# Attention scores in three fp32r products of high and low parts, split on GpSimd, in a fused attention and feed-forward kernel

## The chip, the cores and the metric

One Trainium2 chip, one core. The metric is device time in microseconds of one execution, the median of several runs. Lower is better.

## The reference

Attention with a position bias for 4 batches, 8 heads, 576 positions and 64 features a head, followed by a feed-forward layer with a rational activation. All inputs and the output are float32 in shape and meaning (the feed-forward weights arrive as 64-bit numbers and are converted in the kernel). Cut to what matters here:

```python
scores = scale * np.matmul(q, k.transpose(0, 1, 3, 2))      # (4, 8, 576, 576)
...
scores = scores + bias.transpose(2, 0, 1)[None, :, :, :]
scores = scores - np.max(scores, axis=-1, keepdims=True)
attn = np.exp(scores)
attn = attn / (np.sum(attn, axis=-1, keepdims=True) + 1e-09)
attn_out = np.matmul(attn, v)
...
h = x @ w_in
...
out = g @ w_out                                              # g: a ratio of polynomials of h
```

## The kernel before, in words

The program has two halves. In the first, to about 260 us, the bias table is built (to about 44 us) and then attention is computed. In the second the feed-forward layer runs on TensorE in fp32r, each float32 operand split into a high part (rounded to fp32r) and a low part (the rest), with three products: high by high, high by low, low by high.

Attention is cut into 16 units: a unit is a pair of heads of one batch (`units`). The two heads of a pair lie in the two halves of the 128 partitions, 64 features each. A unit has four blocks of 128 query rows (c = 0 to 3, the full blocks), and the last 64 rows of two neighbouring units share a fifth block (c = 4). So two units make nine steps, and there are 72 steps (`steps`). In the order of one group, counted by the step's number modulo nine, steps 0 to 3 are full blocks of the even unit, step 4 is the shared short block, and 5 to 8 are full blocks of the odd unit. The change concerns `e_qk`, which multiplies q by k for one step: for each half a of the key columns (288 each) and each head j one `T.matmul` in float32 with 64 rows of contraction. A float32 matmul appears in the trace as two records. Each head's scores go to a PSUM tile of their own (`sc`, two tiles in all, so every step uses both again).

What a step issues is written out by hand in `step_a(i)`, engine by engine and in order:

- TensorE: the scores of step i (`e_qk`, L337), the transposes of the exponentials of step i-2 (`e_tp`, L406, and of the sums, L422), the products with v of step i-3 (`e_pv`, L446).
- VectorE: two reductions of step i (`e_ttr`, L347, one per head: adds the bias, scales, finds the extreme, and so empties the score tiles), then, where a unit ends, the sums' reciprocals (`e_recip`, L373 and L374), copies out of PSUM (L425, L429, L456), and one operation of the background job.
- ScalarE: the exponentials (L363) and the copy of the transposes out of PSUM (L414), and one operation of the job.
- GpSimd: the normalization `e_norm` (L395, two in nine steps) and two operations of each job.

The background job converts one block of feed-forward weights (`w_conv`): VectorE masks (`mag`, L140, SBUF to SBUF with a constant), ScalarE rebiases (L149), VectorE puts the sign in (`sign`, L152, two tensors from SBUF) and joins the mantissa (`join`, L165, two tensors from SBUF), GpSimd copies 16-bit halves (`mid`, L161) and subtracts the high from the joined value (`low`, L172, after `join`). `run_jobs` hands out one VectorE operation a step from step 8 on, and with it whatever follows it in the list for the other engines, so a job takes three steps; twenty jobs run in the stage. With L140 handed out in steps 2, 5 and 8 of a group, VectorE runs it after the scores of the next step have started: L140 in steps 0, 3 and 6, L152 in 1, 4 and 7, L165 in 2, 5 and 8.

Each engine runs its instructions in the order of issue. DMAs are issued from SP, in order too. `loads(i)` issues the loads of q and k (`load_qk`): those of the even unit of the next group in step 0, of the odd one in step 5.

Of the kernel before, what the change touches and what calls it, by code (L numbers as in the profile page):

```python
# [8 lines left out]
F32 = mybir.dt.float32  # L9
F32R = mybir.dt.float32r  # L10
U32 = mybir.dt.uint32
AF = mybir.ActivationFunctionType
ALU = mybir.AluOpType
# [3 lines left out]
P = 128  # L17
# [12 lines left out]
SH = S // 2  # L30
# [3 lines left out]
def tile_attn_moe(  # L34
# [79 lines left out]
    def w_conv(f, part):  # L114
        st = {}
        here = f < 6
        eng = G if f < KF - LATE else V

        def load():
            w = (w_in, w_out)[part]  # L120

            def get(nm, o, src):
                t = stg.tile([P, 4 * FN + 4], U16, tag="wx", name=f"{nm}{f}_{part}", bufs=3)
                nc.sync.dma_start(out=t[:, o:o + 4 * FN], in_=src)
                return t

            x = get("wx", 0, w.bitcast(U16)[f])[:, 0:4 * FN]
            st["u"] = x.bitcast(U32).rearrange("p (f t) -> p f t", t=2)[:, :, 1]
            if eng is G:
                st["h"] = x.rearrange("p (f t) -> p f t", t=4)[:, :, 1:3]  # L130
            else:
                y = get("wy", 1, w.bitcast(U16)[f])[:, 2:4 * FN + 2]
                st["m"] = y.bitcast(U32).rearrange("p (f t) -> p f t", t=2)[:, :, 0]

        def tl(nm, dt, bufs=1):
            st[nm] = stg.tile([P, FN], dt, tag=nm, name=f"{nm}{f}_{part}", bufs=bufs)
            return st[nm]

        def mag():
            V.tensor_scalar(  # L140
                out=tl("wk", U32), in0=st["u"], scalar1=0x7FFFFE00, scalar2=None, op0=ALU.bitwise_and
            )

        def rows(t):
            return t.rearrange("p (k f) -> p k f", k=KD)

        def rebias():
            st["wh"] = rows(tl("wh", U32, 2))
            A.activation(out=st["wh"], in_=rows(st["wk"]), func=AF.Relu, bias=wmin, scale=8.0)  # L149

        def sign():
            V.scalar_tensor_tensor(  # L152
                out=st["wh"], in0=rows(st["u"]), scalar=0x80000000, in1=st["wh"],
                op0=ALU.bitwise_and, op1=ALU.bitwise_or,
            )

        def mid():
            if eng is G:
                st["m"] = tl("wm", U32)
                m = st["m"].bitcast(U16).rearrange("p (f t) -> p f t", t=2)  # L160
                G.tensor_copy(out=m, in_=st["h"])  # L161

        def join():
            st["x"] = st["m"] if eng is G else tl("wk", U32)
            V.scalar_tensor_tensor(  # L165
                out=rows(st["x"]), in0=rows(st["m"]), scalar=13, in1=st["wh"],
                op0=ALU.logical_shift_right, op1=ALU.bitwise_or,
            )

        def low():  # L170
            st["wl"] = w_hilo(f, part)[1] if here else rows(tl("wl", F32R, 2))
            eng.tensor_tensor(  # L172
                out=st["wl"], in0=rows(st["x"]).bitcast(F32), in1=st["wh"].bitcast(F32), op=ALU.subtract
            )

        def store(hi=True, lo=True):
            if not here:
                w_out_to(f, part, st["wh"] if hi else None, st["wl"] if lo else None)
            elif hi:
                nc.sync.dma_start(out=w_hilo(f, part)[0].bitcast(F32), in_=st["wh"].bitcast(F32))  # L180

        return [load, [mag], [rebias], [sign, join, low, store], mid]

    def w_plain(f, part):
        st = {}

        def load():
            st["x"] = stg.tile([P, KD, P], F32, tag="wx", name=f"wx{f}_{part}")
            nc.sync.dma_start(out=st["x"], in_=w_src(f, part))

        def hi():
            st["h"] = stg.tile([P, KD, P], F32R, tag="wh", name=f"wh{f}_{part}")
            A.copy(out=st["h"], in_=st["x"])

        def lo():
            st["l"] = stg.tile([P, KD, P], F32R, tag="wl", name=f"wl{f}_{part}")
            V.tensor_tensor(out=st["l"], in0=st["x"], in1=st["h"].bitcast(F32), op=ALU.subtract)

        return [load, [], [hi], [lo, lambda: None, lambda hi=True, lo=True: w_out_to(f, part, st["h"] if hi else None, st["l"] if lo else None)], lambda: None]
# [31 lines left out]
    with tc.manual_schedule():  # L231
# [3 lines left out]
        with ExitStack() as actx:  # L235
# [9 lines left out]
                G.memset(t, 0.0)  # L245

            units = [(p, b) for p in range(NP) for b in range(B)]
            qk = {}
            vt = {}
            bias = {}  # L250

# [10 lines left out]
            def load_qk(u, eng=nc.sync):  # L262
                p, b = units[u]
                q = qkp.tile([P, S], F32, tag="q", name=f"q{u}", bufs=3)
                k = qkp.tile([P, S], F32, tag="k", name=f"k{u}", bufs=3)
                eng.dma_start(out=q, in_=qt[b, p])
                eng.dma_start(out=k, in_=kt[b, p])
                qk[u] = (q, k)

            def load_v(u, eng=nc.sync):  # L270
                p, b = units[u]
                t = vpool.tile([P, 5, P], F32, tag="v", name=f"v{u}")
                eng.dma_start(out=t, in_=vp[b, p])
                vt[u] = t
# [49 lines left out]
            def e_qk(i):  # L324
                u, c = steps[i]
                for j in range(2):
                    sc[i, j] = ps_sc.tile([P, 2, 512], F32, tag="sc", name=f"sc{i}_{j}")
                if c < 4:
                    ops = [(u, slice(c * P, c * P + P), slice(0, P))]
                else:  # L330
                    ops = [(u + z, slice(512, S), slice(64 * z, 64 * z + 64)) for z in range(2)]
                for a in range(2):
                    for j in range(2):
                        r = slice(64 * j, 64 * j + 64)
                        for n, x, o in ops:
                            q, k = qk[n]
                            T.matmul(  # L337
                                sc[i, j][o, a, :SH], q[r, x], k[r, a * SH:(a + 1) * SH],
                                start=True, stop=True,
                            )  # L340

            def e_ttr(i, j):
                u, c = steps[i]
# [54 lines left out]
            def e_tp(i, mx):  # L398
# [16 lines left out]
                last = c == (3 if u % 2 else 4)  # L415
                if last:
                    n = nsum(u)
                    rt = epool.tile([10, P], F32, tag="rt", name=f"rt{u}", bufs=2)
                    rsum[u] = dpool.tile([n, P], F32, tag=f"rs{u}", name=f"rs{u}")
                    for r in range(2):  # L420
                        x = slice(64 * r, 64 * r + 64)
                        T.transpose(mx[:, r, 64:P], sums[u % 4][x, :], ident[x, x])  # L422
# [58 lines left out]
            def loads(i):  # L481
# [5 lines left out]
                        load_v(u)  # L487
                if i == UPG + 1:
                    load_v(3)
                p, r = divmod(i, 2 * UPG)  # L490
                r = {2: 0, 7: 1, 11: 2, 13: 3, 16: 4}.get(r)
                if r is not None and p + 1 < NP:
# [465 lines left out]
```

## Time and profile before

| what | value |
|---|---|
| median of 3 runs | 671.99 us (671.89 to 672.24) |
| span of the profiled execution | 669.7 us |
| busy: TensorE matmul | 663.3 us (99%) |
| busy: VectorE | 569.1 us (85%) |
| busy: ScalarE | 481.7 us (72%) |
| busy: GpSimd | 156.5 us (23%) |
| attention steps | about 44 to 260 us, 2.97 to 3.08 us each |

The span runs from the first to the last instruction that the profiler shows; the device time of the runs holds a little more at either end. A busy share is a mean over the whole span; the attention stage has other shares than the feed-forward half. Records of matmuls are pipelined: the start of one to the start of the next is its price, not its length.

### The profile page before, as it was taken

How to read it: one execution, taken by the hardware profiler on the slowest of the kernel's cores; microseconds unless marked ns; L12 is line 12 of the kernel's file. 1: busy time of each engine (PE TensorE's matmuls, PEld its weight loads, DVE VectorE, ACT ScalarE, POOL GpSimd, SP SyncE). 2: the span in 40 equal slices, each digit the busy share in tenths (PEclk: the TensorE clock that was granted, in tenths of full speed). 3: DMA queues.
4: the chain of work that ended last, by engine and by line, in shares of the span. 5: the costliest groups of instructions: out<-in, count | busy, mean ns of one | idle time of the engine just before them, and what ended most of it. 6: DMA issues, size and time to landing. Idle time of an engine off the chain costs nothing.

```text
span 669.7 us, 16638 instructions
## 1 busy us (share of the span) xinstructions
PE 663.3 (99%) x6466; PEld 574.2 (86%) x6466; DVE 569.1 (85%) x1068; ACT 481.7 (72%) x769; POOL 156.5 (23%) x116
## 2 busy tenths in 40 slices
PE   9999999999999999999999999999999999999997
PEld 6657888888888888999999999999999999999995
DVE  7996888888888895799999999998978787878776
ACT  7978988989898996767676666666655555555561
POOL 0000233334334321122222222222222222222221
PEclk9999999999999999999999999999999999999999
DMA  6886878688688773233644444679621212122021
GB/s 244 305 322 204 308 245 302 219 272 275 226 276 297 233 248 113 100 108 115 220 120 164 132 151 134 197 220 348 249 96 47 95 48 93 50 93 95 1 95 47
DMA packets 74846, 119.01 MB, mean 178 GB/s; under 512 B 11904, under 2 KB 33808, under 8 KB 74768
## 3 DMA queue, kind: packets, MB, share of 16 engines
q1 hardware_dynamic: 74624, 117.79, 53.1%
q8 instruction: 51, 0.84, 0.5%
q14 instruction: 27, 0.22, 0.1%
q10 hardware_dynamic: 144, 0.16, 0.1%
HBM read 79.17 MB, written 35.61 MB: 171 GB/s over the span
## 4 chain that ended last, share of the span: by engine, by line
PE 97%; DVE 1%; issue 1%; ACT 0%; DVEq 0%; POOL 0%; ACTq 0%; POOLq 0%
PE h L313 30%; PE o L788 30%; PE mx L446 13%; PE sc L337 13%; PE tp L406 5%; PE pb L653 4%; DVE ring L614 1%; PE mx L406 1%; PE warm L593 1%; ACT pt L414 0%; PE mx L422 0%; DVE s L347 0%; DVEq L954 0%; ACT p L363 0%; DVEq L614 0%
## 5 line engine op out<-in xcount | busy, mean ns | idle before, releaser
L757 POOL TENSOR_TENSOR gl<-m,r 128x768 fp32r<-128x768 f32 x47 | 87.1, 1853 | 307.6 <-DVE m L750 288.1
L710 ACT ACTIVATE w<-h,babs 128x768 f32<-128x768 f32 x48 | 43.3, 902 | 99.1 <-PE h L313 99.1
L347 DVE CUSTOM_DVE_ANT_0 s<-sc,bias 128x576 f32<-128x576 f32 x144 | 103.2, 753 | 11.9 <-PE sc L337 5.3
L363 ACT ACTIVATE p<-s,m 128x576 f32<-128x576 f32 x144 | 110.7, 772 | 1.6 <-DVE m L347 1.6
L313 PE MATMUL h<-xh,wih 128*128 128x384 f32 x288 | 96.9, 336 | 0.0
L313 PE MATMUL h<-xh,wil 128*128 128x384 f32 x288 | 96.7, 336 | 0.0
L313 PE MATMUL h<-xl,wih 128*128 128x384 f32 x288 | 96.5, 335 | 0.0
L446 PE MATMUL mx<-pt,v 128*64 128x128 f32 (+1 forms) x1600 | 95.1, 267 | 0.0
L337 PE MATMUL sc<-k,q 64*128 64x288 f32 (+1 forms) x640 | 90.6, 426 | 0.5 <-DVE m L347 0.4
L414 ACT COPY pt<-tp 128x1024 f32<-128x1024 f32 x72 | 72.5, 1007 | 24.2 <-PE tp L406 23.8
L788 PE MATMUL o<-wol,gh 128*128 128x512 f32 x216 | 84.7, 392 | 0.0
L788 PE MATMUL o<-woh,gh 128*128 128x512 f32 x216 | 84.6, 392 | 0.0
L446 PEld LDWEIGHTS mx<-pt,v 128*64 128x64 f32 x1600 | 78.5, 137 | 5.0 <-issue 0.3
L720 DVE SCALAR_TENSOR_TENSOR u<-w,babs,h 128x768 f32<-128x768 f32 x48 | 48.6, 1013 | 30.8 <-ACT t L711 30.8
L715 ACT ACTIVATE u<-u 128x768 f32<-128x768 f32 x48 | 40.7, 848 | 41.0 <-DVE u L720 41.0
L337 PEld LDWEIGHTS sc<-k,q 64*128 64x128 f32 (+1 forms) x640 | 49.1, 175 | 20.2 <-DVE m L347 6.9
L736 DVE SCALAR_TENSOR_TENSOR gh<-t,cst,r 128x768 fp32r<-128x768 f32 x48 | 48.6, 1013 | 9.5 <-ACT r L717 7.2
L313 PEld LDWEIGHTS h<-xh,wih 128*128 128x128 f32 x288 | 54.1, 188 | 1.8 <-issue 0.5
L313 PEld LDWEIGHTS h<-xl,wih 128*128 128x128 f32 x288 | 54.1, 188 | 1.3
L788 PE MATMUL o<-woh,gl 128*128 128x512 f32 x216 | 54.8, 389 | 0.0
L313 PEld LDWEIGHTS h<-xh,wil 128*128 128x128 f32 x288 | 54.0, 188 | 0.0
L743 DVE SCALAR_TENSOR_TENSOR m<-u,qc,gh 128x768 f32<-128x768 f32 x48 | 48.9, 1018 | 4.9
(73 smaller groups left out, 1261.4 us busy)
## 6 DMA issues: line engine op xcount, KB each, us to landing
tab<-e SPq DMA_DIRECT2D x36, 295.5 KB, 3.8
wx<-in_w_in_dram SPq DMA_DIRECT2D x16, 512.0 KB, 6.1
wx<-in_w_out_dram SPq DMA_DIRECT2D x16, 512.0 KB, 4.2
xr<-xd SPq DMA_DIRECT2D x7, 768.0 KB, 4.6
v<-in_vp_dram SPq DMA_DIRECT2D x16, 320.0 KB
ws<-wh SPq DMA_DIRECT2D x20, 256.0 KB, 2.0
ws<-wl SPq DMA_DIRECT2D x20, 256.0 KB, 4.3
q<-in_qt_dram SPq DMA_DIRECT2D x16, 288.0 KB
```

The source lines that it names most:

```text
L313: T.matmul(hps[s][:, j, :TT], w[:, k, sl], x[:, k, :], start=(k == 0 and z == 0), stop=(k == KD - 1 and z == 2),)
L337: T.matmul(sc[i, j][o, a, :SH], q[r, x], k[r, a * SH:(a + 1) * SH], start=True, stop=True,)
L347: V.tensor_tensor_reduce(out=t.rearrange("p (a s) -> p a s", a=2), in0=sc.pop((i, j))[:, :, :SH], in1=bias[p][:, 5 * j + c, :].rearrange(" ...
L363: A.activation(out=prob[i][:, z * S:z * S + S], in_=t, func=AF.Exp, bias=m, scale=-1.0, accum_out=sums[u % 4][:, k:k + 1],)
L414: A.copy(out=t[:, 0:8].rearrange("p x (r s) -> p r x s", r=2), in_=ps)
L446: T.matmul(ps[y, o], vt[n][:, kc, y], t[:, 2 * kc + j if kc < 4 else 8, o], start=(kc == 0), stop=(kc == 4),)
L710: A.activation(out=w, in_=h, func=AF.Abs, scale=babs[:, 1:2])
L720: V.scalar_tensor_tensor(out=et(s, "u", 2), in0=rt[s, "w"], scalar=babs[:, 0:1], in1=hps[s][:, :, :TT], op0=ALU.add, op1=ALU.mult,)
L736: V.scalar_tensor_tensor(out=hi, in0=rt[s, "t"], scalar=abs_[:, 0:1], in1=rt[s, "r0"], op0=ALU.add, op1=ALU.mult,)
L743: V.scalar_tensor_tensor(out=m, in0=rt[s, "u"], scalar=qc, in1=rt[s, "gh"].bitcast(F32), op0=ALU.add, op1=ALU.mult,)
L757: eng.tensor_tensor(out=lo, in0=rt[s, "m"], in1=rt[s, "r0"], op=ALU.mult)
L788: T.matmul(po[n, c], l[:, j, c * P:(c + 1) * P], r[fp][:, j, :], start=(first and x is a), stop=(last and x is z),)
```

## The change

In `e_qk`, for full blocks from the third unit on (`c < 4 and u >= 2`), the one float32 product becomes three fp32r products that add up in the same PSUM tile: high q by high k, high q by low k, low q by high k. The short blocks (c = 4) and the first two units stay in float32. The parts are made by the new function `split_qk` on GpSimd: for q and for k of a unit one copy of 128x576 that rounds to fp32r (the high part) and one subtraction (the low part). `loads` calls it in the steps whose number modulo nine is 4 (q of the next group's even unit), 6 (its k), 0 (q of the odd unit of the same group) and 2 (its k), at the head of the step's program. For the space that the parts take, the buffer of the weights' low parts (`wl`) goes from two to one, that of the transposed sums (`rt`) too, and the scratch for descriptors of DMAs is set to 512.

```diff
-            st["wl"] = w_hilo(f, part)[1] if here else rows(tl("wl", F32R, 2))
+            st["wl"] = w_hilo(f, part)[1] if here else rows(tl("wl", F32R))
...
+            def split_qk(u, z):
+                hi = qkp.tile([P, S], F32R, tag=f"h{z}", name=f"h{z}_{u}")
+                lo = qkp.tile([P, S], F32R, tag=f"l{z}", name=f"l{z}_{u}")
+                G.tensor_copy(out=hi, in_=qk[u][z])
+                G.tensor_tensor(out=lo, in0=qk[u][z], in1=hi.bitcast(F32), op=ALU.subtract)
+                hl[u, z] = (hi, lo)
...
+                if c < 4 and u >= 2:
+                    (qh, ql), (kh, kl) = hl[u, 0], hl[u, 1]
+                    passes = [(qh, kh), (qh, kl), (ql, kh)]
+                else:
+                    passes = [None]
                 for a in range(2):
-                    for j in range(2):
-                        r = slice(64 * j, 64 * j + 64)
-                        for n, x, o in ops:
-                            q, k = qk[n]
-                            T.matmul(
-                                sc[i, j][o, a, :SH], q[r, x], k[r, a * SH:(a + 1) * SH],
-                                start=True, stop=True,
-                            )
+                    for y, w in enumerate(passes):
+                        for j in range(2):
+                            r = slice(64 * j, 64 * j + 64)
+                            for n, x, o in ops:
+                                q, k = w or qk[n]
+                                T.matmul(
+                                    sc[i, j][o, a, :SH], q[r, x], k[r, a * SH:(a + 1) * SH],
+                                    start=(y == 0), stop=(y == len(passes) - 1),
+                                )
...
-                    rt = epool.tile([10, P], F32, tag="rt", name=f"rt{u}", bufs=2)
+                    rt = epool.tile([10, P], F32, tag="rt", name=f"rt{u}", bufs=1)
...
+                g, y = divmod(i - 4, UPG)
+                if y in (0, 2, 5, 7):
+                    u = 2 * g + (2 if y < 5 else 3)
+                    if 2 <= u < NU:
+                        split_qk(u, y % 5 // 2)
...
-    nc = bacc.Bacc("TRN2", target_bir_lowering=False, num_devices=1)
+    nc = bacc.Bacc("TRN2", target_bir_lowering=False, num_devices=1, dynamic_dma_scratch_size=512)
```

## Rows read from the trace of the kernel before

**Rows 1.** The page: busy us of the engines; granted TensorE clock in 40 slices.
```profile
PE 663.3 (99%) x6466; PEld 574.2 (86%) x6466; DVE 569.1 (85%) x1068; ACT 481.7 (72%) x769; POOL 156.5 (23%) x116
...
PEclk9999999999999999999999999999999999999999
```

**Rows 2.** Chain that ended last, two steps' scores: start us, us, what.
```profile
206.06 1.17 PE sc L337 x8
...
209.04 1.17 PE sc L337 x8
```

**Rows 3.** Windows view, 60 to 240 us: busy us and instructions of each engine.
```profile
60.00:240.00 180.00, 180.00 (x2978) 149.73 (x2974) 155.10 (x467) 162.19 (x320) 61.39 (x49) 1.00 0.81 262
```

**Rows 4.** Timeline of one step: start us, us, engine, line, operation, idle before.
```profile
205.60 1.41 POOL L395 TENSOR_TENSOR xs<-xs,rb 128x576 f32<-128x576 f32 x1
...
205.99 1.24 PE L337 MATMUL sc<-k,q 64*128 64x288 f32 x8
206.11 0.29 DVE L425 COPY pt<-mx 128x128 f32<-128x128 f32 x1 [0.27 <-PE mx L446]
...
206.52 0.78 DVE L140 TENSOR_SCALAR wk<-wx 128x512 uint32<-128x512 uint32 x1
...
206.58 0.41 PE L337 MATMUL sc<-k,q 64*128 64x288 f32 x2
...
206.83 0.41 PE L337 MATMUL sc<-k,q 64*128 64x288 f32 x2
...
207.38 0.76 DVE L347 CUSTOM_DVE_ANT_0 s<-sc,bias 128x576 f32<-128x576 f32 x1
```

**Rows 5.** Chain that ended last, fp32r products of the feed-forward half.
```profile
325.24 4.18 PE h L313 x24
329.43 4.12 PE o L788 x18
```

**Rows 6.** GpSimd's groups, 60 to 240 us: busy us, mean ns, idle before.
```profile
L161 POOL COPY wm<-wx 128x1024 uint16<-128x1024 uint16 x19 | 20.9, 1099 | 22.8 <-DMA wx<-in_w_in_dram 22.1
L395 POOL TENSOR_TENSOR xs<-xs,rb 128x576 f32<-128x576 f32 x12 | 18.1, 1506 | 0.0
...
L172 POOL TENSOR_TENSOR wil<-wm,wh 128x512 fp32r<-128x512 f32 x6 | 7.7, 1282 | 37.2 <-DVE wm L165 32.0 <-DMA k<-in_kt_dram 5.2
```

**Rows 7.** Lines by themselves: ns min/median/max, first and last start.
```profile
L161 POOL COPY wm<-wx x20: 1036/1036/1248, 68.5 to 242.1; 128x1024 uint16<-128x1024 uint16 x20
...
L140 DVE TENSOR_SCALAR wk<-wx x19: 365/637/1114, 71.4 to 233.6; 128x512 uint32<-128x512 uint32 x19
...
L347 DVE CUSTOM_DVE_ANT_0 s<-sc,bias x144: 739/754/760, 46.0 to 259.5; 128x576 f32<-128x576 f32 x144
...
L373 DVE TENSOR_SCALAR sum<-sum x16: 161/169/676, 68.1 to 261.9; 128x10 f32<-128x10 f32 x8, 128x8 f32<-128x8 f32 x8
```

**Rows 8.** Timeline about 252 us, GpSimd and VectorE.
```profile
251.20 1.41 POOL L395 TENSOR_TENSOR xs<-xs,rb 128x576 f32<-128x576 f32 x1 [0.21 <-DMA rb<-rs]
...
251.91 1.12 DVE L299 TENSOR_TENSOR xl<-xs,xh 128x384 fp32r<-128x384 f32 x1
```

**Rows 9.** Timeline, 230.7 to 234.2 us, VectorE and TensorE.
```profile
230.73 0.69 DVE L165 SCALAR_TENSOR_TENSOR wm<-wm,wh 128x512 uint32<-128x512 uint32 x1
...
231.34 0.55 DVE L299 TENSOR_TENSOR xl<-xr,xh 128x384 fp32r<-128x384 f32 x1
...
231.81 0.75 DVE L347 CUSTOM_DVE_ANT_0 s<-sc,bias 128x576 f32<-128x576 f32 x1
...
233.05 1.24 PE L337 MATMUL sc<-k,q 64*128 64x288 f32 x7
...
234.13 0.40 PE L337 MATMUL sc<-k,q 64*128 64x288 f32 x1
```

**Rows 10.** DMA issues: operation, KB each, median us from issue to landing.
```profile
ws<-wl SPq DMA_DIRECT2D x20, 256.0 KB, 4.3
```

More of the change, by code (lines that the diff above doesn't have):

```diff
@@ L195, in lo @@
         def lo():
-            st["l"] = stg.tile([P, KD, P], F32R, tag="wl", name=f"wl{f}_{part}")
+            st["l"] = stg.tile([P, KD, P], F32R, tag="wl", name=f"wl{f}_{part}", bufs=1)
             V.tensor_tensor(out=st["l"], in0=st["x"], in1=st["h"].bitcast(F32), op=ALU.subtract)
@@ L247, in tile_attn_moe @@
             units = [(p, b) for p in range(NP) for b in range(B)]
-            qk = {}
+            qk, hl = {}, {}
             vt = {}
```

## The prediction

> **What bounds the kernel now.** I read the page first: TensorE is busy 99% of the span and its granted clock is at the upper level, 2.4 GHz, in every slice [rows 1]. The chain that ended last, in order of time, says the same of the stage that is changed: score products, transposes, products with v, and again score products, with nothing between, 2.98 us from one step's scores to the next [rows 2]. So a step costs what TensorE needs for it, and time taken out of the score products is time gained, unless another engine then comes last.
>
> The windows view says how near the others are: in 60 to 240 us VectorE is busy 155 of 180 us, ScalarE 162, GpSimd 61 [rows 3]. The timeline of one step shows the order that matters on VectorE [rows 4]. Scores start at 205.99 (call that T). At 206.11 VectorE, which has waited 0.27 us for the v products, copies the tails; at T+0.53 it runs one operation of the weight-conversion job (here L140); at T+1.39 it begins the two reductions (L347) that empty the score banks. The next scores need those banks. The banks are single, so a late first reduction delays the next scores one for one.
>
> How late may it be? At 230.73 VectorE had two operations to run instead of one; the reduction began at 231.81, and the scores that started at 233.05 had their last product at 234.13, 1.08 us after their start, where 0.84 is normal (206.83 less 205.99) [rows 4, 9]. They were 0.24 us late. So the next scores can be had 1.48 us after the first reduction begins (231.81 + 1.48 = 233.29 = 233.05 + 0.24). Records of VectorE overlap a little where it doesn't wait (L299 ends at 231.89, the reduction starts at 231.81 [rows 9]), so I count 1.41 us from the end of the job operation.
>
> **What the change takes from TensorE.** In float32 one full step has eight records, four pairs of row halves that run side by side; the third pair starts at 206.58 and the fourth at 206.83, a pitch of 0.24 us [rows 4], 0.243 if 0.84 us to the fourth pair are a first load of 0.11 and three pitches. In fp32r it has 2 x 3 x 2 = 12 products, six pairs. The price of an fp32r product is in the second half of the kernel: 24 of 384 columns take 4.18 us, 18 of 512 take 4.12 us [rows 5], so 174 and 229 ns, 0.43 ns a column, and 174 - 96 x 0.43 = 133 ns for 288 columns. Six pairs are 0.80 us where four were 0.97: 0.17 us a step. Bounds: 0.123 us a pair (288 x 0.43 without the fixed part; the float32 pair shows hardly any) gives 0.23; halves that don't overlap cost 12 x 0.133 = 1.60, a loss of 0.63. I take 133 ns: same number format, same chip. Full steps from the third unit on: 14 units x 4 = 56. Gain if nothing else comes last: 56 x 0.17 = 9.5 us.
>
> **What it puts on GpSimd.** Per unit two copies and two subtractions of 128x576. The subtraction has a row of its own size and kind: 1.41 us (L395, undisturbed) [rows 4]. The copy has none: L161 copies 1024 elements in 1.04 us in the median (1.10 in the mean) [rows 6, 7], about 0.67 for 576 by elements allowing 0.15 to 0.2 of fixed cost; a copy as dear as the two-input operation would be 1.41. I take 0.67 and keep both ends. A group of nine steps (two units) gains 4 x 2.08 = 8.3 us of GpSimd work beside today's three L161, three L172 (1.28) and two L395, 10 us [rows 6]: 18 of about 27 us. GpSimd itself is not the bound and the splits are issued three steps ahead of their use.
>
> **What that does to VectorE.** Here is the price that decides. In the stage L140 runs in 0.365 us at best, 0.64 in the median and 1.11 at worst [rows 7]. The step of rows 4 shows why: it was issued at 206.52 while GpSimd's L395 ran from 205.60 to 207.01, and took 0.78, to 207.30, that is 0.29 after L395's end. An operation with two operands in SBUF does the same: L299, 0.55 us at 231.34 [rows 9], took 1.12 at 251.91, with L395 running until 252.61 [rows 8]. The reductions, whose scores come from PSUM, never stretch: 739 to 760 ns over 144 [rows 7]. So a VectorE operation that uses SBUF in this way stands still until GpSimd's current instruction ends. The kernel's other job operations, L152 and L165 (0.68 us), have two SBUF operands as L299 has, and in this trace they never met a GpSimd instruction; I price them as L299. The Trainium skill, page "SBUF — State Buffer", section "Who interferes with whom", states this as an exclusive lock: the later of the two engines blocks fully, for one-source VectorE operations in their two-port modes and for ones with two SBUF inputs against GpSimd reads. The trace agrees for L140 and L299 (0.29 and 0.42 us after L395's end); no row shows it for L152 and L165, and by the page they block too, which is the forecast below and not the first rival.
>
> Replay of nine steps, with T8 = 0, jobs due at T+0.53, copy 0.67, and the shortened step 2.80 (2.85 where sums are transposed, 3.04 for the step of short rows, which stays float32). Step 8: L165 ends at 1.21; GpSimd runs L172 to 2.53, L395 to 3.94. Step 0 (T = 2.80): L140 waits until 3.94, ends 4.28, next scores at 5.69, 0.09 late. GpSimd: L161 to 5.32, copy to 5.99; L373, one-source too and seen at 0.16 to 0.68 us [rows 7], waits for it and ends at 6.16; subtraction to 7.57. Step 1 (5.69): L152 waits to 7.57, ends 8.25, next scores 9.66, 1.17 late. Step 2: L165 is free, L172 to 12.2, copy to 12.87, subtraction to 14.28. Step 3 (12.51): L140 waits to 14.28, next scores 16.0, 0.69 late. L161 to 15.64, L395 to 17.05. Step 4: L152 waits to 17.05, ends 17.73, next scores 19.14, 0.10 late. Copy and subtraction to 19.81, L165 waits a little, no loss, T6 = 21.94. L172, L161 to 22.85; L373 waits for it, the copy comes between (to 23.69), L140 ends 24.02, T7 = 25.43, 0.64 late. Step 7 is clear; T8 again at 28.3. Before, nine steps took 9 x 2.97 plus 0.3 for the dearer ones, 27.05. So a group gets 1.25 us longer: 2.7 lost, 8 x 0.17 = 1.4 gained. Six groups hold both splits and jobs: +7.5. In the last nine steps the jobs run out (sixty operations from step 8 on), so they keep their gain of 1.4. **Sum: +6.1 us.** The profiled span of 669.7 lies 2.3 us under the median of 671.99; the rest lies around it and is not touched. 671.99 + 6.1 = 678.1.
>
> The places of the collisions hang on a tenth of a microsecond (in step 3, copy first or L140 first), the sum less: with the copy at 0.5 to 0.9 the same replay gives +3 to +8, with 1.41 a group of 30.5 us and +19.
>
> **Edits that cost nothing.** Low parts of the weights have one buffer: their store lands in 4.3 us [rows 10] and the next one is written three steps (9 us) later; without that slack L172 would wait on the store, GpSimd's splits behind it. The single sum buffer is written every four to five steps. More scores wait on GpSimd now: behind them on TensorE stands everything, but the split is three steps (8 us) ahead, and GpSimd has 8 us a group free. The DMA scratch size moves no instruction. ScalarE needs 2.68 us a step (162/180 of 2.98 [rows 2, 3]), which a step of 2.80 still covers, with little left.
>
> **Rivals.** (1) Only one-source operations (L140, L373) stand still, L152 and L165 don't: the losses of steps 1 and 4 go (1.27 a group), and that of step 3 may, which leaves 0.7 to 1.4 lost against 1.4 gained: 6 x (-0.7 to 0) - 1.4 = -5.6 to -1.4, middle 668.5. For it: L152 and L165 have no row. Against: L299. (2) The collisions stay away, since GpSimd falls out of step with the jobs: -9.5 us, 662.5, down to 659 at 0.12 us a pair. Against: GpSimd will be two thirds busy, and at today's one third L140 already stretches in more than half of its runs [rows 7]. (3) The two row halves don't run side by side in fp32r: +0.63 x 56 = +35, 707. It decides as soon as a pair costs over 0.162 us. Only float32 rows show halves side by side. (4) Gain and loss cancel within 0.2% (1.3 us, about what a measurement of this kernel can tell from no change).
>
> **Numbers.** Main case, slower by 1.4 to 19 us, 0.62; rival 1 0.14, of which I count 0.02 within 0.2%; rival 2 0.14; rival 3 0.05; rival 4 0.05. Faster 0.26, same 0.07, slower 0.67. The range leaves out rival 3, most of the copy's dear end and the best of rival 2: 664.5 to 687.
>
> **What would show it.** L337 in fp32r with pairs at 0.13 us; GpSimd busy some 110 us in 60 to 240 us where it was 61; L140, L152 and L165 stretched to 1 to 2 us with a GpSimd instruction ending 0.3 to 0.7 us before their end; TensorE idle before L337, put down to L347; the stage some 6 us longer and the second half unchanged. Wrong if L152 and L165 stay at 0.68 beside a running GpSimd, or if the copy is so short or so placed that the waits fall in VectorE's idle time.

## The result and the profile after

The changed kernel takes 680.74 us (679.18 to 681.67, four runs) where the kernel before took 672.09 in the same series: ratio 1.0127, 95% interval 1.0113 to 1.0141, 8.65 us slower. The prediction was 678.1, between 664.5 and 687.

The page after, busy us of the engines and the granted clock, and the windows view of 60 to 240 us:

```profile
PE 665.6 (98%) x6690; PEld 582.0 (86%) x6690; DVE 587.9 (87%) x1068; ACT 483.0 (71%) x769; POOL 217.2 (32%) x172
...
PEclk9999999999999999999999999999999999999999
```
```profile
60.00:240.00 180.00, 176.60 (x3108) 152.81 (x3104) 164.69 (x450) 158.58 (x311) 115.21 (x100) 1.00 0.80 257
```

The clock is still at the upper level (2.4 GHz) in every slice. TensorE, which was never idle in 60 to 240 us [rows 3], now stands idle for 3.4 of these 180 us. GpSimd is busy 115 us where it was 61, and VectorE 165 where it was 155, with fewer instructions in the window (450, were 467): the same work, stretched.

TensorE's own gain is there, to the size. The timeline of one full step's scores, one row for each pair of products:

```profile
172.65 0.40 PE L350 MATMUL sc<-h,h 64*128 64x288 f32 x2
172.89 0.30 PE L350 MATMUL sc<-l,h 64*128 64x288 f32 x2
173.02 0.29 PE L350 MATMUL sc<-h,l 64*128 64x288 f32 x2
173.15 0.30 PE L350 MATMUL sc<-h,h 64*128 64x288 f32 x2
173.29 0.29 PE L350 MATMUL sc<-l,h 64*128 64x288 f32 x2
173.42 0.29 PE L350 MATMUL sc<-h,l 64*128 64x288 f32 x2
```

From 172.89 to 173.42 there are four pitches of 0.133 us, and the two row halves share a pitch, so they run side by side. That is the forecast's price for a pair. Where nothing else comes last, the start of one step's scores to the next is now 2.79 us (99.03 to 101.82, steps 18 and 19), where it was 2.98 [rows 2].

Where the time went shows on VectorE. Lines by themselves, ns min/median/max (the first three with first and last start in us; L140 and L360 are the lines L140 and L347 of before [rows 7], L152 and L386 the sign and the sums' constant):

```profile
L140 DVE TENSOR_SCALAR wk<-wx x20: 417/989/1593, 72.1 to 250.0; 128x512 uint32<-128x512 uint32 x20
...
L152 DVE SCALAR_TENSOR_TENSOR wh<-wx,wh x20: 669/1136/1691, 75.1 to 255.2; 128x512 uint32<-128x512 uint32 x20
...
L386 DVE TENSOR_SCALAR sum<-sum x15: 256/403/1414, 68.7 to 260.0; 128x10 f32<-128x10 f32 x8, 128x8 f32<-128x8 f32 x7
...
L360 DVE CUSTOM_DVE_ANT_0 s<-sc,bias x128: 696/746/758, 60.5 to 259.3; 128x576 f32<-128x576 f32 x128
```

L140's median went from 0.64 to 0.99 us, L152, which took 669 to 685 ns before, has a median of 1.14, and the reductions kept their length. The timeline of VectorE, and then that of GpSimd, in the first steps of a group shows why:

```profile
99.55 0.97 DVE L140 TENSOR_SCALAR wk<-wx 128x512 uint32<-128x512 uint32 x1
100.45 0.74 DVE L360 CUSTOM_DVE_ANT_0 s<-sc,bias 128x576 f32<-128x576 f32 x1
...
102.57 1.52 DVE L152 SCALAR_TENSOR_TENSOR wh<-wx,wh 128x512 uint32<-128x512 uint32 x1
104.01 0.74 DVE L360 CUSTOM_DVE_ANT_0 s<-sc,bias 128x576 f32<-128x576 f32 x1
...
108.80 1.59 DVE L140 TENSOR_SCALAR wk<-wx 128x512 uint32<-128x512 uint32 x1
...
112.07 1.14 DVE L152 SCALAR_TENSOR_TENSOR wh<-wx,wh 128x512 uint32<-128x512 uint32 x1
```
```profile
98.82 1.42 POOL L408 TENSOR_TENSOR xs<-xs,rb 128x576 f32<-128x576 f32 x1
...
102.11 1.42 POOL L274 TENSOR_TENSOR l<-q,h 128x576 fp32r<-128x576 f32 x1
...
108.68 1.43 POOL L274 TENSOR_TENSOR l<-k,h 128x576 fp32r<-128x576 f32 x1
...
111.25 1.40 POOL L408 TENSOR_TENSOR xs<-xs,rb 128x576 f32<-128x576 f32 x1
112.60 1.13 POOL L273 CAST h<-q 128x576 fp32r<-128x576 f32 x1
```

Read each VectorE row against the GpSimd row that runs when it starts. L140 at 99.55 ends at 100.52, 0.28 us after L408; L152 at 102.57 ends at 104.09, 0.56 after the subtraction L274; L140 at 108.80 ends 0.28 after L274; L152 at 112.07 ends 0.56 after L408. The reduction follows each of them at once, and the next scores wait for it. These places return every 27.5 us.

To see where in the stage the time is lost I take the start of the first reduction of each step, as at 100.45 in the timeline above, against the same step of the kernel before. Step 18 there, from its timeline of VectorE:

```profile
99.15 0.76 DVE L347 CUSTOM_DVE_ANT_0 s<-sc,bias 128x576 f32<-128x576 f32 x1
```

The changed kernel is 1.3 us late there, 2.8 us late at step 54, and 9.4 us late at the last step, 71. So the four groups between steps 18 and 54 lose 0.38 us each, and the last seventeen steps lose 6.6 us: 2.6 from step 54 to 63, and 4.0 from there to 71. Nothing is added behind the stage: the two spans differ by 9.5 us (679.2 and 669.7).

What holds the steps from 54 to 63 up stands in the waits view of 198 to 270 us (us in total, times, longest) and in the timelines of GpSimd, SP and VectorE:

```profile
POOL wl L172 <- DMA ws<-wl: 10.9, 2, 5.5
```
```profile
198.67 1.28 POOL L172 TENSOR_TENSOR wl<-wm,wh 128x512 fp32r<-128x512 f32 x1 [0.97 <-DVE wm L165]
...
201.74 1.47 POOL L274 TENSOR_TENSOR l<-k,h 128x576 fp32r<-128x576 f32 x1
208.62 1.28 POOL L172 TENSOR_TENSOR wl<-wm,wh 128x512 fp32r<-128x512 f32 x1 [5.41 <-DMA ws<-wl]
209.86 1.61 POOL L408 TENSOR_TENSOR xs<-xs,rb 128x576 f32<-128x576 f32 x1
...
220.44 1.27 POOL L172 TENSOR_TENSOR wl<-wm,wh 128x512 fp32r<-128x512 f32 x1 [5.49 <-DMA ws<-wl]
```
```profile
200.47 0.46 SPq L112 DMA_DIRECT2D ws<-wh  x1
200.99 0.42 SPq L124 DMA_DIRECT2D wx<-in_w_in_dram  x1
201.52 0.40 SPq L266 DMA_DIRECT2D q<-in_qt_dram  x1
201.96 0.45 SPq L267 DMA_DIRECT2D k<-in_kt_dram  x1
202.83 1.35 SPq L112 DMA_DIRECT2D ws<-wl  x1
```
```profile
206.79 0.68 DVE L165 SCALAR_TENSOR_TENSOR wm<-wm,wh 128x512 uint32<-128x512 uint32 x1
...
215.95 0.67 DVE L165 SCALAR_TENSOR_TENSOR wm<-wm,wh 128x512 uint32<-128x512 uint32 x1
```

GpSimd finished a low part at 199.95. SP issued its store at 202.83, behind the store of the high part and three loads, and the store had landed when L172 could write the single buffer again, at 208.62. GpSimd stood still for 5.4 us, but not all of that is the store's: L172 also needs what L165 writes, and L165 ended at 207.47. Elsewhere in this trace L172 starts 0.1 us after L165's end where it waits for L165 alone, so the store held it up by 1.1 us here and by 3.7 at 220.44 (L165 ended at 216.62), 4.8 of the 10.9 us that the view puts down to it. Behind it stood a normalization and splits. After the second wait GpSimd worked them off in a row, and VectorE met them one after another. The timeline of VectorE there:

```profile
225.29 1.88 DVE L165 SCALAR_TENSOR_TENSOR wm<-wm,wh 128x512 uint32<-128x512 uint32 x1 [0.70 <-POOL wm L161]
...
229.38 1.32 DVE L140 TENSOR_SCALAR wk<-wx 128x512 uint32<-128x512 uint32 x1
```

From step 63 on it is something else. Splits are still made there (until step 65), and VectorE also splits x in these steps (L306, L299 before, two tensors from SBUF). The timelines of VectorE and GpSimd:

```profile
243.50 1.77 DVE L306 TENSOR_TENSOR xl<-xr,xh 128x384 fp32r<-128x384 f32 x1
```
```profile
243.06 1.79 POOL L274 TENSOR_TENSOR l<-q,h 128x576 fp32r<-128x576 f32 x1
```

This operation takes 0.55 us where it stands behind nothing (L299 at 231.34 in [rows 9]); here it ends 0.42 us after L274, as it did after L395 in [rows 8].

### The profile page after: what moved, and what is told of

It reads as the page before. It is cut to its first block, busy times and chain, and to the rows that moved or that the text cites. A ratio compares the mean times of both kernels' runs of the same rounds, so it can differ in the third digit from the quotient of the medians.

```text
span 679.2 us, 17160 instructions
## 1 busy us (share of the span) xinstructions
PE 665.6 (98%) x6690; PEld 582.0 (86%) x6690; DVE 587.9 (87%) x1068; ACT 483.0 (71%) x769; POOL 217.2 (32%) x172
## 4 chain that ended last, share of the span: by engine, by line
PE 65%; DMA 4%; DVE 3%; POOL 2%; issue 1%; SPq 1%; ACT 0%; DVEq 0%; POOLq 0%; ACTq 0%
PE h L320 30%; PE o L806 29%; PE mx L459 3%; PE sc L350 2%; PE tp L419 1%; DMA rb<-rs 1%; DVE s L360 1%; DMA ws<-wl 1%; DMA wx<-in_w_in_dram 1%; POOL xs L408 1%; DMA k<-in_kt_dram 1%; DMA ws<-wh 1%; POOL wm L161 0%; DVE xl L306 0%; POOL wl L172 0%
## 5 line engine op out<-in xcount | busy, mean ns | idle before, releaser
L360 DVE CUSTOM_DVE_ANT_0 s<-sc,bias 128x576 f32<-128x576 f32 x144 | 102.7, 749 | 7.3 <-PE sc L350 4.1
L350 PE MATMUL sc<-h,h 64*128 64x288 f32 x224 | 46.9, 344 | 4.1 <-DVE m L360 4.1
L320 PE MATMUL h<-xh,wg 128*128 128x384 f32 x192 | 50.9, 335 | 0.0
```

The source lines that it names most:

```text
L320: T.matmul(hps[s][:, j, :TT], w[:, k, sl], x[:, k, :], start=(k == 0 and z == 0), stop=(k == KD - 1 and z == 2),)
L350: T.matmul(sc[i, j][o, a, :SH], q[r, x], k[r, a * SH:(a + 1) * SH], start=(y == 0), stop=(y == len(passes) - 1),)
L360: V.tensor_tensor_reduce(out=t.rearrange("p (a s) -> p a s", a=2), in0=sc.pop((i, j))[:, :, :SH], in1=bias[p][:, 5 * j + c, :].rearrange(" ...
```

## The experiments

Twelve kernels ran besides the change. For each I give the runs' median and its ratio to the kernel before in the same series, and, from its profiled execution, the shift of the first reductions against before: at step 18, per group of nine between steps 18 and 54, and from step 54 to 71 (us). The column at 18 holds waits for loads too, which differ between kernels: e6_before_low_one, which splits nothing, got its 1.4 in steps 5 to 7, after a wait of 2.1 us for a bias load at step 5.

| kernel | median | ratio, 95% interval | at 18 | per group | 54 to 71 |
|---|---|---|---|---|---|
| the change | 680.74 | 1.0127 (1.0113 to 1.0141) | +1.3 | +0.38 | +6.6 |
| e1_no_split | 668.71 | 0.9951 (0.9936 to 0.9966) | +1.7 | -1.08 | +0.8 |
| e2_split_only | 681.64 | 1.0143 (1.0128 to 1.0158) | +1.0 | +0.67 | +6.4 |
| e3_write_only | 682.83 | 1.0165 (1.0142 to 1.0189) | +1.1 | +1.32 | +4.0 |
| e4_pieces | 677.73 | 1.0079 (1.0054 to 1.0104) | +0.2 | -0.09 | +7.1 |
| e5a_low_one | 682.28 | 1.0155 (1.0140 to 1.0171) | +0.5 | +0.17 | +5.7 |
| e5b_low_two | 679.86 | 1.0113 (1.0098 to 1.0128) | +0.1 | +0.24 | +2.4 |
| e6_before_low_one | 672.78 | 1.0009 (1.0000 to 1.0019) | +1.4 | +0.05 | +0.3 |
| e7_gated | 669.84 | 0.9969 (0.9956 to 0.9982) | +1.5 | -1.06 | +4.2 |
| e8_gated_two | 707.77 | 1.0531 (1.0506 to 1.0557) | +9.8 | +4.85 | +7.2 |
| e9_gated_f32 | 684.20 | 1.0181 (1.0167 to 1.0195) | +5.2 | 0.00 | +8.6 |
| e10_gated_early | 669.12 | 0.9960 (0.9947 to 0.9972) | -0.1 | -1.07 | +3.5 |
| e11_gated_act | 670.35 | 0.9980 (0.9965 to 0.9996) | -1.0 | -1.06 | +3.5 |

**No split.** Units from the fifth on reuse the parts of units 2 and 3, so GpSimd's splits are left out while TensorE's products stay.

```diff
-                    (qh, ql), (kh, kl) = hl[u, 0], hl[u, 1]
+                    (qh, ql), (kh, kl) = hl[2 + u % 2, 0], hl[2 + u % 2, 1]
...
-                    if 2 <= u < NU:
+                    if 2 <= u < 4:
```

> The three products stay, GpSimd splits only units 3 and 4 (the third and fourth); every later unit multiplies the parts of those two, so the scores of later units are those of other data. Theory (VectorE stands still behind GpSimd's split instructions): the extra waits go and only TensorE's gain is left, 56 steps x 0.17 = 9.5 us: 662.5 us, L152 back to 0.68 us. Rival (the three products themselves or their waits cost time, the splits are innocent): 677 to 681.

The sign came out as the theory has it, the size short of it: 3.4 us faster, not 9.5. A group gains 1.08 us; with 0.17 us off each of its eight full steps it would be 1.4. Part of the rest is L140 behind the normalization in the first step of a group (1.05 us at 125.85, 0.99 at 151.85), which the longer float32 scores hid; the remainder was not broken down. Before step 18, where the splits of units 2 and 3 stay, the kernel falls 1.7 us behind.

**Split only.** The parts are made, but all scores use the float32 products.

```diff
-                if c < 4 and u >= 2:
+                if False:
```

> GpSimd splits as in the changed kernel, but all scores stay float32 products, so nothing on TensorE waits for a split or uses one. Theory: VectorE still stands behind the splits, L140 and L152 up to 1.6 us, and as the float32 step has 0.17 us more of slack the loss is a little below that of the changed kernel: 680.7 + 9.5 less up to 56 x 0.17, that is 680 to 688 us. Rival (what costs is TensorE waiting for parts, or fp32r with row halves): 672.

As the theory: 9.5 us slower. The splits alone make a group 0.67 us longer and cost 6.4 us in the last seventeen steps, the same as with the shorter products. GpSimd's wait for the low parts' store is there too (12.1 us in two, of which 4.4 after L165).

**Write only.** GpSimd fills the two parts twice over (128x1152 each time) instead of splitting: it runs as often and longer, but reads nothing from SBUF. The products use the filled parts.

```diff
-                G.tensor_copy(out=hi, in_=qk[u][z])
-                G.tensor_tensor(out=lo, in0=qk[u][z], in1=hi.bitcast(F32), op=ALU.subtract)
+                for x in range(2):
+                    G.memset(t.bitcast(F32), 0.25)
```

> The four split instructions of a unit become four fills of 128x1152 with a constant, about 1.05 us each and 2.1 us for q or k as before, which write SBUF and read none of it; the scores of full blocks from the third unit on are then of constants. If any GpSimd instruction holds up VectorE: as the changed kernel, 677 to 681 us, L152 stretched. If operations with two SBUF operands wait only for GpSimd instructions that read SBUF (the page SBUF - State Buffer of the Trainium skill says so): L152 and L165 beside a fill stay at 0.68, L140 still stretches to about 1.4: 664 to 670 us.

The rows answer, the total doesn't. VectorE and then GpSimd in three places of this kernel's timeline (lines behind the split are one lower than after):

```profile
102.79 0.68 DVE L152 SCALAR_TENSOR_TENSOR wh<-wx,wh 128x512 uint32<-128x512 uint32 x1
...
111.23 1.74 DVE L152 SCALAR_TENSOR_TENSOR wh<-wx,wh 128x512 uint32<-128x512 uint32 x1
...
117.69 1.18 DVE L385 TENSOR_SCALAR sum<-sum 128x10 f32<-128x10 f32 x1
...
119.04 1.20 DVE L140 TENSOR_SCALAR wk<-wx 128x512 uint32<-128x512 uint32 x1
```
```profile
101.20 2.17 POOL L273 MEMSET h<- 128x1152 f32 x2
...
111.01 1.41 POOL L407 TENSOR_TENSOR xs<-xs,rb 128x576 f32<-128x576 f32 x1
...
117.78 2.18 POOL L273 MEMSET h<- 128x1152 f32 x2
```

L152, which has two operands in SBUF, runs beside a fill in its usual 0.68 us and stands still only behind L407, which reads SBUF. L140 and L385, which read one tensor, wait for fills as well: L140 ends 0.28 us after the second fill. Both wait in the same step here, one fill each, and the fills are longer than what they replace, so a group got 1.32 us longer and the total 10.7: against its forecast of 664 to 670 us the run is a miss. So the two kinds of VectorE operation wait on different things, and changing the splits into writes only trades one collision for another. The Trainium skill, page "SBUF — State Buffer", section "Who interferes with whom", states that a VectorE instruction with two SBUF inputs contends with GpSimd instructions that read SBUF and not with those that only write; these rows agree.

The end of this stage fits that too: from step 63 to 71 this kernel loses nothing (-0.1 us), where the change loses 4.0. VectorE's split of x (L305 here) keeps its 0.54 us beside a fill:

```profile
254.34 0.54 DVE L305 TENSOR_TENSOR xl<-xr,xh 128x384 fp32r<-128x384 f32 x1
```
```profile
253.08 2.33 POOL L273 MEMSET h<- 128x1152 f32 x2
```

**Pieces.** The copy in two pieces, the subtraction in four, so that a waiting VectorE operation has less to wait for.

```diff
-                G.tensor_copy(out=hi, in_=qk[u][z])
-                G.tensor_tensor(out=lo, in0=qk[u][z], in1=hi.bitcast(F32), op=ALU.subtract)
+                for x in range(0, S, 288):
+                    G.tensor_copy(out=hi[:, x:x + 288], in_=qk[u][z][:, x:x + 288])
+                for x in range(0, S, 144):
+                    w = slice(x, x + 144)
+                    G.tensor_tensor(out=lo[:, w], in0=qk[u][z][:, w], in1=hi[:, w].bitcast(F32), op=ALU.subtract)
```

> Each copy in two pieces of 288 columns, each subtraction in four of 144: the same work in instructions of 0.3 to 0.5 us. Theory (VectorE waits until GpSimd's current instruction ends): the longest wait behind a split falls from 1.4 to 0.5 us, of which a step hides 0.1 to 0.2; the waits behind L395, L172 and L161 stay: 665 to 672 us. Rival (VectorE loses to GpSimd's busy time, however it is cut): 680 to 684, since the pieces add GpSimd time.

The total lies between the theory (665 to 672) and the rival (680 to 684), and so misses both. A group loses 0.47 us less than with the change (-0.09 against +0.38), and the timeline of VectorE shows that the length of the instruction in flight is what it waits for:

```profile
101.71 0.77 DVE L152 SCALAR_TENSOR_TENSOR wh<-wx,wh 128x512 uint32<-128x512 uint32 x1
```

That is L152 beside the pieces of a subtraction (100.99 to 103.29), where the whole one made it 1.52. Waits behind the whole copies of the words and the normalization stay, and one of them grew: step 6 of a group takes 1.02 us more than before (0.41 with the change), since L140 now meets the whole copy L161 there. The end of the stage is as dear as with the change (7.1 and 6.6 us).

**One low buffer or two.** A second buffer for the weights' low parts has no room in the changed kernel. In both of these the parts of q keep only the 512 columns that are used and two padding tiles are left out; the second of them spends the room on the buffer, the first is its control.

```diff
-            st["wl"] = w_hilo(f, part)[1] if here else rows(tl("wl", F32R))
+            st["wl"] = w_hilo(f, part)[1] if here else rows(tl("wl", F32R, 2))
```

> A control for the next run: the changed kernel with the parts of q cut to the 512 columns that the full blocks use and two small padding tiles left out, which makes room for a second buffer; the low parts of the weights keep one buffer. In the traces so far five middle groups got only 0.4 us longer each, and the last thirteen steps 6.6 us in all, after GpSimd's L172 had waited 5 us, twice, for the store of the low part before. Theory (that wait starts the loss at the end): 678 to 681 us, with the waits of L172 on that store.

> As the control, with two buffers for the low parts of the weights, as before the change. Theory (the single buffer makes L172 wait, which puts GpSimd's later work, splits included, out of step and against VectorE's work at the end of the stage): most of the 6.6 us at the end goes, 674 to 676 us, and no wait of L172 on that store. Rival (the end of the stage loses because VectorE has more SBUF work there, the splits of x, whatever the buffer): as the control within 1 us.

The pair differs by 2.4 us in the medians, 3.3 us in the spans (680.3 and 677.0), and the profile has the difference where it should be: 5.7 us lost in the last seventeen steps with one buffer, 2.4 with two, and no wait of the low parts' subtraction for the store. Both totals miss their forecasts (678 to 681 and 674 to 676). All of the difference falls before step 63 (3.7 and 0.4 us from step 54); from 63 to 71 both lose the same (1.9 and 2.1), and there splits of x run on VectorE. The control itself is not slower in the stage than the change (6.8 us late at its end, where the change is 9.4), but 3.8 us slower after it: its span is 10.6 over that of before. Why is open; the kernel differs from the change in the tiles left out and the shorter parts of q.

**Before with one low buffer.** The kernel before with that one edit of the change.

```diff
-            st["wl"] = w_hilo(f, part)[1] if here else rows(tl("wl", F32R, 2))
+            st["wl"] = w_hilo(f, part)[1] if here else rows(tl("wl", F32R))
```

> The kernel before with one buffer for the low parts of the weights and no other change. If the edit costs nothing by itself, as the prediction said: 672 us. If the wait of L172 on the store is there without the splits and matters: up to 675 us.

The medians differ by 0.75 us (672.78 and 672.03). The waits view puts 14.3 us in two on the store, more than with the change, but L165 ended only 0.4 and 2.4 us before L172 began, so the store itself held L172 up by 2.7 us, where it was 4.8 with the change. And no split is queued behind it here. So the buffer costs under 1 us by itself and some 3 us together with the splits; how much of that is the longer delay and how much the splits behind it is not told apart.

**Gated.** The change, with GpSimd's splits and normalizations issued at the end of a step, behind a copy of one column of what VectorE's job operation of that step wrote. So GpSimd starts a long instruction only when that operation is done, and has the reductions' time (1.5 us) for it. The copy of the words moves behind the subtraction of the job before.

```diff
+            def after_job():
+                if made:
+                    G.tensor_copy(out=gate[:, 0:1], in_=made.pop()[:, 0:1])
...
+                y, m = divmod(i, UPG)
+                if m in (0, 2, 5, 6) and i < NS:
+                    u = 2 * y + (1 if m < 5 else 2)
+                    if 2 <= u < NU:
+                        after_job()
+                        split_qk(u, {0: 0, 2: 1, 5: 0, 6: 1}[m])
```

> The changed kernel with GpSimd's work put where VectorE reduces: each split and each normalization is issued at the end of a step, behind a copy of one column of what VectorE's job operation of that step writes, so it starts when that operation is done; the 16-bit copy of the next job follows the subtraction of the job before it, in place of running beside L140. Parts of q and k are made in steps 0, 2, 5 and 6 of a group in place of 4, 6, 0 and 2. The low parts keep one buffer. Theory (time lost is VectorE standing behind GpSimd): L140 and L152 nearly as when alone (0.37, 0.68), middle groups 25.7 to 26.2 us in place of 27.5, in all 664 to 671 us, the more the less the end loses. Rival (GpSimd's busy time as such, or fp32r, costs): 677 us and more.

It is faster than both kernels, 2.2 us under the kernel before and 10.9 under the change by the medians. The timelines of GpSimd and of VectorE in one step:

```profile
109.40 0.19 POOL L256 COPY gate<-wk 128x1 uint32<-128x1 uint32 x1 [0.34 <-DVE wk L141]
109.52 0.67 POOL L284 CAST h<-k 128x576 fp32r<-128x576 f32 x1
110.27 1.42 POOL L285 TENSOR_TENSOR l<-k,h 128x576 fp32r<-128x576 f32 x1
```
```profile
108.57 0.77 DVE L141 TENSOR_SCALAR wk<-wx 128x512 uint32<-128x512 uint32 x1
109.26 0.74 DVE L371 CUSTOM_DVE_ANT_0 s<-sc,bias 128x576 f32<-128x576 f32 x1
...
111.36 0.87 DVE L154 SCALAR_TENSOR_TENSOR wh<-wx,wh 128x512 uint32<-128x512 uint32 x1
```

The copy and the subtraction run under the reductions, which they don't touch, and L154 (L152 after) is 0.2 us longer than its 0.68 us, where behind a whole subtraction it was 1.52. A group gains 1.06 us, as much as without any split (1.08). What the profiled execution still loses is 2.1 us at step 9, where TensorE waits for the first split, and 4.2 in the last steps. That execution was the slowest of ten (672.98, 3.1 over the median), so the others lose less, and where they do is not on record.

**Gated with two low buffers, and its control in float32.** Room for the second buffer is taken from q and k (two buffers, were three), which moves their loads to the sixth step of a group. The control has the same loads, buffers and gated normalization and plain float32 scores without splits.

```diff
-                q = qkp.tile([P, S], F32, tag="q", name=f"q{u}", bufs=3)
+                q = qkp.tile([P, S], F32, tag="q", name=f"q{u}", bufs=2)
...
-                for u, x, y in ((2 * g + 2, 0 if g else 4, 3 if g else 6), (2 * g + 3, 5 if g else 7, 8)):
+                for u, x, y in ((2 * g + 2, 5, 3 if g else 6), (2 * g + 3, 5, 8)):
```

> The gated kernel with two buffers for the low part of a weight block. Their space comes from q and k, which keep two buffers where they had three: both of a group's next units load at its sixth step (unit 2 on ScalarE's queue, unit 3 at step 9), and the first of them is split behind its seventh and eighth steps. Theory: what the gated kernel still lost was 2.1 us at step 9, where TensorE waited for the first split, and 3.8 us at steps 58 and 59, behind the store of the one buffer. Without these waits 663 to 667 us, and the first reductions of steps 54 to 64 stand no later against those of before than at step 53. Rival 1: the last steps lose to the splits of x and to the other stores, whatever the buffers: 668 to 671. Rival 2: with two buffers q and k land too late for their splits, and TensorE waits for them in every group: over 672.

> As the gated kernel with two buffers, but no unit is split and all scores are plain float32 products; buffers, loads and the gated norm stay. Theory: the gain comes from TensorE's shorter scores, so without them 671 to 673 us, as the kernel before, with groups of 27.0 us. Rival: it comes from the order (norm behind VectorE's job, the copy of the words after the subtraction): within 1 us of its partner.

The first went as its second rival: q lands too late, and TensorE waits in every group from step 18 to step 54. GpSimd's timeline at such a place:

```profile
97.77 0.19 POOL L256 COPY gate<-wh 128x1 uint32<-128x1 uint32 x1 [3.24 <-DVE wh L154]
100.18 0.98 POOL L284 CAST h<-q 128x576 fp32r<-128x576 f32 x1 [2.22 <-DMA q<-in_qt_dram]
```

The first step of each group from step 18 to step 54 took 5.9 to 9.5 us where 3.0 is normal. TensorE's granted clock fell after such waits as well. From 134 to 138 us TensorE was busy for 1.1 us; from 138 to 140 the granted clock was 0.50 (1.2 GHz), and the pairs of score products came 0.24 us apart where 0.133 is normal. So part of the loss is slower work behind the waits. Whether a second low buffer would help the gated kernel stays open, since this one paid for it with late loads. The control missed its total as well, by the moved loads (5.2 us before step 18) and by its end (8.6 us), with clocks of 0.94 in 60 to 90 and 220 to 260 us, so the totals don't compare. Its groups do (clock 1.00 in 90 to 220): 0.00 us against before, with everything of the order in place. What a gated group gains comes from the products.

**Gated, with an early first load, and the low store on ScalarE's queue.**

```diff
-                for u, x, y in ((2 * g + 2, 0 if g else 4, 3 if g else 6), (2 * g + 3, 5 if g else 7, 8)):
+                for u, x, y in ((2 * g + 2, 0 if g else 1, 3 if g else 6), (2 * g + 3, 5 if g else 7, 8)):
```

and in the second also

```diff
-            end = [("sp", x) for x in [lambda st=store: st(False, True)] + after.get(i, [])]
+            end = [("act", lambda st=store: st(False, True))] + [("sp", x) for x in after.get(i, [])]
```

> The gated kernel with the loads of unit 2's q and k issued at step 1 where it issues them at step 4, so that they no longer stand behind twelve bias loads on SP's queue; nothing else moves. Theory: its step 9 then takes 2.9 to 3.2 us where the gated kernel took 5.28, and the time falls by 1.5 to 2.5 us, to 667 to 668.5. Rival: the early transfers delay the first steps by as much, or TensorE waits at step 9 for GpSimd's copies in any case: 669 to 671.

> The same, and the store of a weight block's low part, where it goes to DRAM, is issued on ScalarE's queue instead of SP's, before the next job's exponent step would follow it. Theory: steps 58 and 59 took 9.3 us in the gated kernel because that store stood behind bias loads and row sums on SP and GpSimd waited 4.7 us for its single buffer; on ScalarE's queue it lands some 3 us earlier, and the time falls by another 1.5 to 3.5 us, to 664 to 667. Rival: ScalarE then waits for GpSimd's subtraction, the exponentials stand behind it, and the steps from 47 on grow: 669 or more.

The early load takes the wait at step 9 away (2.97 us, was 5.28), but the median is 669.12, within the spread of the gated kernel's runs (668.05 to 672.98): its worth in the total is not told apart, and the forecast (667 to 668.5) is missed. The store on ScalarE's queue gains nothing: step 58 falls to 2.9 us, but step 59 still takes 4.1 and step 60 grows to 3.9, the subtraction (L175 here) begins 1.2 us late behind a store, one job later, and the median is 670.35, where 664 to 667 was forecast.

## Why the prediction was right, and where it was off

The direction and the mechanism held. That the time came out only 2.6 us over the forecast is luck, since it is the sum of two terms that were off in opposite ways.

- **TensorE's gain.** Right: 0.133 us a pair, row halves side by side, so 0.17 us a step. Rival 3 is out.
- **GpSimd's prices.** Right: the copy takes 0.67 us undisturbed, as worked out by elements from L161, and the subtraction 1.41 to 1.47. GpSimd is busy 115 us in 60 to 240, where some 110 were forecast.
- **VectorE behind GpSimd.** Right: L140, L152 and L386 stretch, and the reductions don't. L165, which the signs named too, met nothing in the groups in the middle, as in the replay. Rival 1 fell with L152's 1.52 us behind a subtraction. The write-only kernel shows what L152 waits for, instructions that read SBUF, and that L140 waits for fills too.
- **The sum of a group.** The places of the collisions were those of the replay, the loss was over-sized: 1.25 us a group was forecast, 0.38 measured, that is 1.8 lost and 1.4 gained where 2.7 and 1.4 were forecast. By the starts of TensorE's scores from step 27 to 36, with the 0.17 us of each shortened step added back, L152 behind a subtraction (step 1) cost 0.82 us where 1.17 were forecast, steps 3 and 4 together 0.70 where it was 0.79, step 6 0.30 where it was 0.64, and step 0 nothing where it was 0.09. In step 1 of the group at 99 us the subtraction ended 1.71 us after the scores' start (101.82 to 103.53), where the replay had 1.88, and L152 0.56 us behind it, where the replay had 0.68.
- **The last eighteen steps.** They were to lose 1.25 us in the sixth group and to gain 1.4 in the last nine steps; they lost 2.6 to step 63 and 4.0 from there to step 71. Two steps of the prediction failed. The first stands under "Edits that cost nothing": the low parts' single buffer was taken as written three steps after its store, which lands in 4.3 us. The store landed 8.7 us after L172 had ended (199.95 to 208.62), since SP issued it 2.9 us late and it took 5.8. The text named the condition ("without that slack L172 would wait on the store, GpSimd's splits behind it") and then gave it no price. The two-buffer pair puts 2.4 to 3.3 us on it, all of it before step 63. The second is "in the last nine steps the jobs run out": sixty operations from step 8 on last to step 67, and splits are made until step 65, so the collisions go on there. VectorE's splits of x, which the prediction had seen wait behind L395 [rows 8], have no place in the replay. The loss from step 63 on stays with two buffers (2.1 us). Without splits the last seventeen steps lose 0.8 in all, and with fills in their place the steps from 63 on lose nothing. That it is VectorE's splits of x, with L140 and L386, meeting GpSimd's work is read from these timelines and was not tried alone.
- **Rival 2**, the collisions stay away, is what the gated kernel makes of the change: its groups gain what they gain without splits. It didn't come by itself.

So 6 x 1.25 - 1.4 = +6.1 became about 1.3 before step 18, 4 x 0.38 = 1.5 to step 54 and 6.6 to the end: 9.4 us in the profiled execution.

## What to carry to other kernels

Work given to an engine with time to spare is not free where its instructions hold up those of a busy one: price each of its instructions at what it holds up when it starts at the wrong moment, and look for the stretch in which the busy engine does something that doesn't mind, here the reductions from PSUM. One cheap instruction that depends on the busy engine's last conflicting operation puts the work there. A buffer taken away elsewhere to make room belongs in the sum: ask how late its store is issued, in the queue that it stands in, and what is queued behind the engine that will wait for it. And a wait that a view puts down to the last of several releasers is not that one's price: take off what the others would have cost in any case.

## What was not expected of the hardware

- The wait goes both ways: GpSimd's copy at 112.60, issued while L152 still ran, took 1.13 us where 0.67 is its undisturbed time.
- An operation on eight or ten columns waits as long as one on 512: L386 took 1414 ns at worst, where the same line took 161 at best before [rows 7].
- In the gated kernel with late loads a wait of TensorE cost more than its own length: the granted clock was 0.92 in the mean of 60 to 240 us, where the change has 1.00.
